# A gate fold in four column groups, with the order of the work computed from new keys

## The chip, the cores and the metric

One core of one Trainium2 chip runs the kernel in one launch. The metric is the device time of that launch in microseconds; less is better. A profile of one execution gives the times of single instructions on the five engines: PE (TensorE; PEld is its weight load), DVE (VectorE), ACT (ScalarE), POOL (GpSimd) and SP (SyncE, which here issues DMAs).

## The reference, cut to what matters

```python
# attention, 2 batches x 8 heads x 768 x 64: a window of 16 around each query and 24 block summaries
x = attention(q, k, v)                                  # 1536 x 512
h = np.maximum(np.maximum(x @ w1, x @ w2), x @ w3)      # 512 -> 768, float64 weights
x2 = h @ w_out                                          # 768 -> 512, float64 weights
# second layer: skip score, 8 experts of 512 -> 1024 -> 512
skip = x2 @ w_skip
e = argmax(x2 @ w_gate); gate = max(softmax(x2 @ w_gate))
out = x2;  out[skip > 0] += gate * (relu(x2 @ m1[e]) @ m2[e])
```

## The kernel before, in words

The tokens are worked in four groups of 384 (u = 0 to 3), each with four pairs of heads (p). For each (u, p) the attention runs scores (sc, `scores`), a reduction on DVE (tt), exponentials on ACT (ex), a reciprocal on DVE (rc), a normalisation on POOL (nm), transposes on PE (tu), a copy (td, on ACT or DVE) and the value product (pv), which ACT and DVE split into a high and a low fp32r part (ph, pl). Each group then has 18 "chains" (c, `chain`, line 413): 12 matmuls each, three products (high by high, high by low, low by high) over four 128-row parts. Their results are combined on ACT and DVE (cd), split on ACT (hh, line 427) and on POOL (hl, line 430), and six f parts of h go into x2 (`x2_mm`, line 440).

The weights of the first layer come as 64-bit floats in 24 pieces (`weight_order`). Each is converted in eight steps: c1 and cq on ACT (lines 385, 381), cb on POOL (line 389), c2, which is two instructions, and c3 on DVE (lines 393, 394, 398), c4, a cast on ACT or POOL (line 402), and c5 on DVE (line 406). Conversion tiles named cx have four slots, and tiles named cr two.

The gate fold. The router needs x2 @ [w_gate, w_skip], ten columns with one of zeros. The kernel puts these columns behind w_out: for each of the six 128-row pieces (3, f) of w_out it computes the 128 x 10 product of that piece with the gate weights, and x2 then has 522 columns. A fold is: `fold_t` (ft), four PE transposes of the piece into PSUM (line 478); `fold_c` (fc), an ACT copy of 128x512 into a cr tile (line 483); `fold_mm` (fm), four matmuls (line 489), each with a transposed 128x128 part as the stationary operand and the ten gate columns (w9) as the moving one, summed in PSUM; `fold_h` (fh, ACT, line 494) and `fold_l` (fl, DVE, line 497), which write the ten columns' high and low parts behind the weights. All six folds must be done before x2 of group 0. The matmul of fm is fp32, and each of the four shows as two instructions in the trace.

The order of the work up to the first expert tile is computed at build time: `arrange` (line 93) walks a list of operations with an engine, a planned duration, predecessors (`after`), buffer slots that an operation takes and gives back (`take`, `uses`), and a key. Whenever an engine is free, the ready operation with the lowest key whose slots are free goes next. The result is the order of each engine's in-order instruction stream; the planned durations and the keys set nothing else. The keys are the table KEYS; one row holds the keys of the folds (f), one those of the 24 conversions (w), one those of the chains (c), one those of the weight loads (l), and so on. The table HOME says which of the movable copies run on which engine: 11 of the 24 c4 casts on POOL, 4 of the 32 td copies on DVE. KIND sorts PE's operations; where two that follow each other are of different kinds, the plan charges PE a small switch.

The PSUM pool psM has three slots, which chains, x2, the transposes and the folds share. The tiles t1 have five slots, and each h tile one. An h tile of group 1 can only be written once x2 of group 0 has read it, so chains of group 1 can run ahead of x2 of group 0 by a few f parts only.

After the planned part (its first expert matmuls are at line 1164) the expert tiles run in an order written out by hand: pairs of tiles (`pair`), single ones (`single`), and a tail tile of 32-token parts (`tail`), whose matmuls (lines 1097 and 1108) have 32 stationary columns and write four column groups of PSUM partitions.

Of the kernel before, what the change touches and what calls it, by code (L numbers as in the profile page):

```python
# [19 lines left out]
P = 128  # L20
# [11 lines left out]
KC1 = DM // P  # L32
FT1 = DF // P
NE, FF = 8, 1024
CAP = 1664
NROW = NE * CAP
NT = B * S // P
SEQ = 24
# [4 lines left out]
MAXT = NT  # L43
ONES, DENSE, OTHER = 32, 64, 128
NRAW = 4
NCON = 293
NG9 = 10
XW = DM + NG9
XA = XW // 2 + 1
# [1 line left out]
TICK, COLUMNS = 10.24 / 3, 3500  # L51
RATE = dict(sc=973, pv=1516, fm=200)
PORT = ("rc", "fk", "c2", "c3", "c5", "tri")
KIND = dict(ch=0, cp=0, x2m=0, sc=1, pv=2, tu=3, st=3, ft=3, fm=1, wu=5)
PORTED, SWITCH = 0.5, 0.06

KEYS = dict(
    s=[[92.73, -181.27, -146.9, -16.72], [12.35, 16.72, 8.44, 74.05], [153.96, 186.16, 209.64, 168.62],
       [133.34, 186.33, 278.0, 31.35]],
    t=[[-48.88, -30.72, -72.46, -64.96], [-115.16, -107.84, -74.91, -96.18], [166.13, 294.76, 153.99, 200.69],  # L60
       [231.34, 228.77, 194.22, 148.78]],
    o=[[-192.26, -99.49, -155.84, -140.77], [18.47, 16.47, 41.51, 37.81], [199.26, 186.19, 169.77, 161.26],
       [233.93, 202.13, 203.99, 188.4]],
    v=[[-76.04, -20.69, -43.67, -52.86], [-21.73, 66.33, 25.77, 62.78], [184.33, 170.84, 129.72, 69.28],
       [217.41, 88.27, 101.06, 155.42]],
    d=[[-190.77, -106.26, -79.61, -70.3], [14.18, 17.1, 46.42, 50.54], [166.48, 205.9, 182.89, 208.26],
       [219.14, 230.09, 253.13, 240.15]],
    e=[[-118.48, -161.65, -267.53, -240.31], [-154.8, -98.57, -105.32, -102.62], [120.29, 131.21, 115.09,
       112.64], [172.38, 173.49, 165.52, 214.6]],
    c=[[23.72, 3.57, 54.8, 22.22, 44.87, 43.88, 88.26, 54.59, 86.07, 36.89, 6.99, -26.57, -32.31, 15.28,  # L70
# [5 lines left out]
    x=[-95.61, 258.36, 184.11, 502.78],  # L76
    w=[18.99, -6.3, 51.7, 43.13, 14.1, 99.04, 74.8, 61.7, 81.52, 99.86, 64.82, 35.29, 63.01, 76.52, 58.72,
       87.44, 90.17, 111.95, 78.35, 139.2, 88.06, 51.57, 155.3, 161.2],
    l=[-91.01, -34.87, 30.81, -0.24, -49.37, 13.11, 15.41, -9.33, 19.62, 18.83, 49.47, 74.71, 132.91, 84.56,
       70.49, 102.42, 139.84, 87.62, 100.63, 192.14, 145.35, 197.7, 185.22, 170.88],  # L80
    f=[61.9, 116.3, 154.03, 120.79, 115.82, 130.96],
)
KEYS = {(z,) + ((n, i) if isinstance(x, list) else (n,)): y for z, v in KEYS.items() for n, x in enumerate(v)
        for i, y in enumerate(x if isinstance(x, list) else [x])}
HOME = {
# [3 lines left out]
}  # L89
HOME = {(n, i): e for (n, e), v in HOME.items() for i in v}  # L90

# [103 lines left out]
def build(tc, a, out):  # L195
    nc = tc.nc
    ctx = ExitStack()
    cp = ctx.enter_context(tc.tile_pool(name="const", bufs=1))
# [22 lines left out]
    KS, VS, XH, XL, WH, WL, HH, HL, LG, X2, ST = ({} for _ in range(11))  # L221
# [264 lines left out]
    def fold_mm(f):  # L486
        pg = psM.tile([P, 512], F32, name="pm")
        for c in range(KC1):
            nc.tensor.matmul(pg[:, :NG9], ST["ft", f][:, c * P:(c + 1) * P], w9[:, c, :], start=(c == 0),  # L489
                             stop=(c == KC1 - 1))  # L490
        ST["fg", f] = pg

    def fold_h(f):
        nc.scalar.copy(WH[3, f][:, DM:], ST["fg", f][:, :NG9])
# [2 lines left out]
        nc.vector.tensor_tensor(WL[3, f][:, DM:], ST["fg", f][:, :NG9], WH[3, f][:, DM:].bitcast(F32), ALU.subtract)  # L497

    con = cp.tile([P, NCON], F32, name="con")
    parts = np.split(np.arange(NCON), np.cumsum([KC1 * NG9, NE, NE, NE, NE * NE, SEQ, NT, 1]))  # L500
    w9, iom, iocap, ione, trie, seqc, tok, quart, tri32 = (con[:, z[0]:z[-1] + 1] for z in parts)
    w9 = w9.rearrange("p (c e) -> p c e", e=NG9)
    trie = trie[:1].rearrange("p (a b) -> p a b", b=NE)
    seqc = seqc[:1]
    tri = cp.tile([P, P], BF16, name="tri")
# [351 lines left out]
    def op(name, eng, dur, key, fn, *args, after=(), take=(), uses=(), lag=0.0):  # L857
        key = (key.name, key.more) if isinstance(key, at) else (None, key)
        busy = eng == "Pool" and lag == 0 and dur > 0 and name[0] != "rs"
        OPS.append(dict(name=name, eng=eng, dur=dur, key=key, fn=fn, args=args, after=after, take=take, uses=uses,  # L860
                        lag=lag, busy=busy))
# [55 lines left out]
    for i in range(20):  # L917
        n = 6 if i == 0 else 3
        op(("wu", i), "PE", 0.216 * n, 1.0 * i, warm_up, n, after=[("wu", i - 1)] if i else [],
           take=[("pm", ("wu", i))] + ([("t1", ("wt",))] if i == 0 else []),  # L920
           uses=[("wu", i)] + ([("wt",)] if i == 19 else []))
    for p in range(NPR):
        att(0, p)
    for n, (j, f) in enumerate(ws):
        t, w = at("w", n), (j, f)
# [8 lines left out]
    for f in range(FT1):  # L934
        t, w = at("f", f), (3, f)
        op(("ft", f), "PE", 0.6, t, fold_t, f, after=[("c3",) + w], take=[("pm", ("ft", f))], uses=[("cx",) + w])
        op(("fc", f), "ACT", 0.48, t + 0.1, fold_c, f, after=[("ft", f)], take=[("cr", ("fc", f))], uses=[("ft", f)])
        op(("fm", f), "PE", 0.9, t + 0.2, fold_mm, f, after=[("fc", f), ("consts",)], take=[("pm", ("fm", f))], uses=[("fc", f)])
        op(("fh", f), "ACT", 0.07, t + 0.3, fold_h, f, after=[("fm", f), ("c4",) + w])
        op(("fl", f), "DVE", 0.1, t + 0.4, fold_l, f, after=[("fh", f), ("c5",) + w], uses=[("fm", f)])  # L940
    for u in range(NG):
        if u + 1 < NG:
# [3 lines left out]
        for k in range(3 * FT1):  # L946
            f, j = divmod(k, 3)
            t, c = at("c", u, k), (u, f, j)
# [4 lines left out]
            for z in range(KC1 - 1 if sp else 0):  # L953
                op(("cp", z) + c, "PE", 0.55, t, chain, u, f, j, [z], after=[("pl", 0, z), ("c5", j, f)] + ([("cp", z - 1) + c] if z else []),
                   take=[] if z else [("pm", ("ch",) + c)])
            if sp:
                dep += [("cp", KC1 - 2) + c]
            op(("ch",) + c, "PE", 0.55 if sp else 2.1, t + 0.01, chain, u, f, j, [KC1 - 1] if sp else range(KC1), after=dep,
               take=[] if sp else [("pm", ("ch",) + c)],
               uses=[("xh", u), ("xl", u)] if k == 3 * FT1 - 1 else [])  # L960
            if j == 0:
                op(("cd",) + c, "ACT", 0.43, t + 0.1, chained, u, f, j, after=[("ch",) + c], take=[("t1", ("t1", u, f))],
                   uses=[("ch",) + c])
            else:
# [15 lines left out]
        if not g3:  # L980
            for t in range(TPG):
                x = x0 + 2 * t
# [5 lines left out]
                else:  # L988
# [3 lines left out]
                   uses=[("x2p", u, t, 0)])  # L992
                op(("xo", u, t, 1), "ACT", 0.28, x + 1.1, x2_out, u, t, 1, after=[d1, ("xo", u, t, 0)])
                op(("lg", u, t), "DVE", 0.1, x + 1.2, x2_lg, u, t, after=[("xo", u, t, 1)] + ([("lg", u, t - 1)] if t else []),
                   uses=[("x2p", u, t, 1)])
                op(("xd", u, t, 0), "DMA", 0.75, x + 1.3, x2_put, u, t, out, after=[("xo", u, t, 1)])
                op(("xd", u, t, 1), "DMA", 0.75, x + 1.4, x2_put, u, t, x2d, after=[("xd", u, t, 0)], uses=[("X2", u, t)])
        else:
            x = x0
            mm(0, 1, 0, x)  # L1000
            d = [mm(0, 1, 1, x + 0.2), mm(1, 1, 2, x + 1), mm(2, 1, 2, x + 2)]
# [421 lines left out]
def host_inputs(inputs):  # L1423
    q, k, v = inputs["q"], inputs["k"], inputs["v"]
    r = {}
# [28 lines left out]
    r["m1"], r["m2"] = inputs["moe2_w1"], inputs["moe2_w2"]  # L1454
    w9 = np.concatenate([inputs["moe2_w_gate"], inputs["moe2_w_skip"][:, None], np.zeros((DM, 1), np.float32)], axis=1)
    w9 = w9.reshape(KC1, P, NG9).transpose(1, 0, 2).reshape(P, KC1 * NG9)
    e = np.arange(NE, dtype=np.float32)
    trie = (e[None, :] < e[:, None]).astype(np.float32)
    same = np.concatenate([e - NE, e * CAP, e, trie.ravel(), np.arange(SEQ, dtype=np.float32)])
    tok = np.arange(B * S, dtype=np.float32).reshape(NT, P).T  # L1460
    quart = (np.arange(P) // TAIL).astype(np.float32)[:, None]
    r["con"] = np.concatenate([w9, np.tile(same, (P, 1)), tok, quart, np.triu(np.ones((P, P), np.float32), 1)], axis=1)
    assert r["con"].shape == (P, NCON)
    return r

# [15 lines left out]
```

## Time and profile before

| what | value |
|---|---|
| median of 3 runs | 456.3 us (454.33 to 458.5) |
| profiled execution, time | 457.91 us |
| its span, first to last instruction | 456.1 us |
| mean granted TensorE clock | 0.984 |
| PE busy | 438.1 us (96%) |
| DVE, ACT, POOL busy | 239.6, 187.1, 141.6 us |

The profiled execution takes 1.8 us more than its span, and 1.6 us more than the median of the runs. A granted clock of 1.00 is 2.4 GHz, 0.50 is 1.2 GHz. Ends of matmuls in the trace are modelled; so the distance between two starts says more about PE than the durations do.

### The profile page before, as it was taken

The numbers are of one execution on the slowest core, as the hardware profiler recorded it, in microseconds if no ns is written. First come the engines' busy times: TensorE is split into PE (matmuls) and PEld (weight loads), VectorE is DVE, ScalarE is ACT, GpSimd is POOL, SyncE is SP. The second block draws the span as 40 slices with busy tenths as digits, with TensorE's granted clock in tenths as the row PEclk, the third lists the DMA queues.
The fourth block names the chain that finished last, engine by engine and source line by source line (L and its number), as shares of the span: only waits on it lengthen the run. The fifth ranks groups of instructions, "written<-read, shape, count | busy, mean of one in ns | idle before, by whom it ended". The sixth has DMA issues, their size and how long they took to land.

```text
span 456.1 us, 9606 instructions
## 1 busy us (share of the span) xinstructions
PE 438.1 (96%) x3546; PEld 396.2 (87%) x3546; DVE 239.6 (53%) x735; ACT 187.1 (41%) x504; POOL 141.6 (31%) x191
## 2 busy tenths in 40 slices
PE   5999899999999998999999999999999999999995
PEld 2767789999999888999999998998999889799875
DVE  3689899999730743315312338658316752221321
ACT  2788887455461575724121126312123521211210
POOL 2464456325211541203320235041326134130400
PEclk9799999999979999999999999999999999999999
DMA  8964735678112346331003038122762184110101
GB/s 246 299 227 130 245 105 177 217 243 282 49 39 92 133 114 151 102 119 47 2 1 139 0 107 311 47 94 47 239 224 93 29 291 148 26 39 13 46 31 49
DMA packets 27585, 56.91 MB, mean 125 GB/s; under 512 B 6099, under 2 KB 8659, under 8 KB 27528
## 3 DMA queue, kind: packets, MB, share of 16 engines
q1 hardware_dynamic: 24968, 50.24, 34.2%
q0 software_dynamic: 2560, 5.96, 4.1%
q8 instruction: 30, 0.49, 0.5%
q14 instruction: 27, 0.22, 0.2%
HBM read 46.69 MB, written 10.47 MB: 125 GB/s over the span
## 4 chain that ended last, share of the span: by engine, by line
PE 83%; DVE 6%; DMA 3%; issue 2%; POOL 1%; ACT 1%; SPq 1%; POOLq 0%; ACTq 0%; DVEq 0%
PE pm L413 27%; PE ph L1164 13%; PE pm L1176 12%; PE pm L440 11%; DMA qt<-in_qt 3%; PE ph L1257 2%; PE po L354 2%; PE pt L341 2%; PE pm L235 2%; PE sc L302 2%; PE pm L489 1%; PE pm L1229 1%; DVE cx L398 1%; PE ptx L776 1%; PE pm L1299 1%
## 5 line engine op out<-in xcount | busy, mean ns | idle before, releaser
L413 PE MATMUL pm<-xh,wh 128*128 128x384 f32 x288 | 65.2, 346 | 0.7 <-DVE t L422 0.4
L413 PE MATMUL pm<-xl,wh 128*128 128x384 f32 x288 | 62.3, 336 | 0.3 <-DVE xl L365 0.3
L413 PE MATMUL pm<-xh,wl 128*128 128x384 f32 x288 | 62.2, 335 | 0.0
L413 PEld LDWEIGHTS pm<-xh,wh 128*128 128x128 f32 x288 | 49.6, 188 | 2.7 <-DVE t L422 1.2
L413 PEld LDWEIGHTS pm<-xl,wh 128*128 128x128 f32 x288 | 51.2, 188 | 0.7 <-DVE xl L365 0.6
L1167 ACT ACTIVATE hth<-ph 128x256 fp32r<-128x256 f32 x40 | 15.3, 384 | 87.6 <-PE ph L1164 81.8
L413 PEld LDWEIGHTS pm<-xh,wl 128*128 128x128 f32 x288 | 51.1, 188 | 0.0
L1168 DVE SCALAR_TENSOR_TENSOR htl<-ph,hth 128x256 fp32r<-128x256 f32 x40 | 16.9, 423 | 57.3 <-ACT hth L1167 57.3
L440 PE MATMUL pm<-wh,h 128*128 128x262 f32 (+1 forms) x288 | 43.4, 292 | 1.8 <-ACT h L427 0.6
L336 POOL TENSOR_TENSOR pr<-pr,se 128x360 f32<-128x360 f32 x32 | 26.5, 845 | 56.2 <-DVE se L332 45.0
L422 DVE TENSOR_TENSOR t<-pm,t 128x384 f32<-128x384 f32 x48 | 26.4, 552 | 32.2 <-PE pm L413 23.0
L326 ACT ACTIVATE pr<-pr,mx 128x120 f32<-128x120 f32 x96 | 36.6, 384 | 15.3 <-DVE mx L319 15.1
L440 PEld LDWEIGHTS pm<-wh,h 128*128 128x128 f32 x288 | 39.0, 195 | 2.9 <-ACT t L420 0.8
L430 POOL TENSOR_TENSOR h<-t,h 128x384 fp32r<-128x384 f32 x24 | 25.8, 1079 | 35.8 <-ACT h L427 25.7
L1176 PE MATMUL pm<-wh,hth 128*128 128x512 f32 x80 | 31.7, 396 | 0.0
L1176 PE MATMUL pm<-wl,hth 128*128 128x512 f32 x80 | 31.5, 393 | 0.0
L1176 PE MATMUL pm<-wh,htl 128*128 128x512 f32 x80 | 31.5, 393 | 0.0
L789 POOL DMA_INDIRECT xn<-x2d,inx x14 | 15.5, 1109 | 45.7 <-DVE xm L1130 30.8
L607 POOL DMA_INDIRECT table<-rtab,rsi x12 | 12.0, 1001 | 55.6 <-DVE g_m L625 20.7
L1164 PE MATMUL ph<-xth,wh 128*128 128x256 f32 x160 | 26.4, 287 | 0.0
L389 POOL TENSOR_SCALAR cx<-cx 128x512 f32<-128x512 f32 x24 | 19.0, 793 | 22.4 <-ACT cx L385 22.1
L1164 PE MATMUL ph<-xtl,wh 128*128 128x256 f32 x160 | 25.7, 282 | 0.0
(333 smaller groups left out, 856.1 us busy)
## 6 DMA issues: line engine op xcount, KB each, us to landing
raw<-in_m SPq DMA_DIRECT2D x48, 256.0 KB
raw<-in_wx SPq DMA_DIRECT2D x22, 512.0 KB
vx<-in_vx SPq DMA_DIRECT2D x14, 288.0 KB
qt<-in_qt SPq DMA_DIRECT2D x16, 192.0 KB
raw<-in_vt SPq DMA_DIRECT2D x8, 384.0 KB
x2d<-raw SPq DMA_DIRECT2D x12, 256.0 KB
kx<-in_kx SPq DMA_DIRECT2D x8, 360.0 KB
out<-raw SPq DMA_DIRECT2D x9, 256.0 KB
```

Of the source, the lines that this page charges most:

```text
L326: nc.scalar.activation(pr[:, t, :], pr[:, t, :], AF.Exp, bias=mx[:, t:t + 1], scale=-1.0, accum_out=se[:, h, t:t + 1])
L336: nc.gpsimd.tensor_tensor(pr, pr, ST["se", u, p][:, h].unsqueeze(2).broadcast_to([P, TPG, KT]), ALU.mult)
L389: nc.gpsimd.tensor_scalar(x, x, HIGH, LOW, ALU.min, ALU.max)
L413: nc.tensor.matmul(ST["ch", u, f, j], l[j, f][:, c * P:(c + 1) * P], r[u][:, c, :], start=(cs[0] == 0 and n == 0), stop=(cs[-1] == KC1 - 1 ...
L422: nc.vector.tensor_tensor(ST["t1", u, f], ps, ST["t1", u, f], ALU.max)
L430: nc.gpsimd.tensor_tensor(HL[u, f], ST["t1", u, f], HH[u, f].bitcast(F32), ALU.subtract)
L440: nc.tensor.matmul(ps, l[u, f][:, t * P:(t + 1) * P], r[3, f][:, lo:hi], start=(part != 1 and n == 0), stop=(part != 0 and n == len(ops) - 1))
L789: nc.gpsimd.indirect_dma_start(out=xn[t], out_offset=None, in_=x2d, in_offset=bass.IndirectOffsetOnAxis(ap=inx[:, t, 0:1], axis=0), bounds ...
L1164: nc.tensor.matmul(ps, w[:, o:o + P], r[:, d, :], start=(n == 0), stop=(n == 3 * KC1 - 1))
L1167: nc.scalar.activation(hh, ps, AF.Relu)
L1168: nc.vector.scalar_tensor_tensor(hl, ps, 0.0, hh.bitcast(F32), ALU.max, ALU.subtract)
L1176: nc.tensor.matmul(py[i], l[:, o:o + P], r, start=(f == 0 and n == 0), stop=(f == 7 and n == 2))
```

## The change

fold_mm swaps the operands: 32 columns of the constants (the ten gate columns of a 128-row part, and 22 columns that follow) are the stationary operand and the transposed piece is the moving one, 128 columns wide. The four parts go to four groups of 32 PSUM partitions, each with a product of its own. A new ACT copy (fs) brings the 128x128 result to the first quarter of the same cr tile, and a new matmul (fq) with a constant 0/1 matrix (pick9, ten more columns of the constants) adds the four parts and turns them to 128 x 10, in another stretch of the same PSUM slot. The cr tile is given back after fq. fh waits for fq in place of fm. The planned durations of the fold change with it, all keys are new, three of the 11 POOL casts go to ACT on balance (five of POOL's move to ACT, two of ACT's to POOL), and td has five copies on DVE in place of four, two of them the same.

```diff
-NCON = 293
+NCON = 303
-KIND = dict(ch=0, cp=0, x2m=0, sc=1, pv=2, tu=3, st=3, ft=3, fm=1, wu=5)
+KIND = dict(ch=0, cp=0, x2m=0, sc=1, pv=2, tu=3, st=3, ft=3, fm=1, fq=1, wu=5)
...
-    w=[18.99, -6.3, 51.7, 43.13, 14.1, 99.04, 74.8, 61.7, 81.52, 99.86, 64.82, 35.29, 63.01, 76.52, 58.72,
-       87.44, 90.17, 111.95, 78.35, 139.2, 88.06, 51.57, 155.3, 161.2],
+    w=[29.12, -32.19, 57.18, 48.36, -2.78, 108.08, 79.78, 61.39, 111.49, 132.7, 74.37, 38.77, 66.75, 74.46,
+       56.98, 94.39, 121.93, 130.7, 84.22, 176.38, 71.77, 45.85, 164.69, 225.48],
...
-    f=[61.9, 116.3, 154.03, 120.79, 115.82, 130.96],
+    f=[60.9, 119.7, 155.29, 122.03, 119.18, 158.31],
...
-    ("c4", "Pool"): [0, 1, 3, 6, 8, 9, 14, 17, 21, 22, 23],
+    ("c4", "Pool"): [0, 1, 3, 6, 8, 16, 19, 22],
     ("fv", "Pool"): [(0, 1), (0, 2), (0, 3)],
-    ("td", "DVE"): [(0, 0, 1), (1, 0, 0), (1, 1, 0), (1, 3, 1)],
+    ("td", "DVE"): [(0, 0, 0), (1, 0, 0), (1, 1, 1), (1, 2, 1), (1, 3, 1)],
...
     def fold_mm(f):
         pg = psM.tile([P, 512], F32, name="pm")
         for c in range(KC1):
-            nc.tensor.matmul(pg[:, :NG9], ST["ft", f][:, c * P:(c + 1) * P], w9[:, c, :], start=(c == 0),
-                             stop=(c == KC1 - 1))
+            nc.tensor.matmul(pg[32 * c:32 * c + 32, :P], con[:, c * NG9:c * NG9 + 32], ST["ft", f][:, c * P:(c + 1) * P], start=True, stop=True)
         ST["fg", f] = pg
+
+    def fold_s(f):
+        nc.scalar.copy(ST["ft", f][:, :P], ST["fg", f][:, :P])
+
+    def fold_q(f):
+        ST["fg", f] = ST["fg", f][:, 2 * P:]
+        nc.tensor.matmul(ST["fg", f][:, :NG9], ST["ft", f][:, :P], pick9, start=True, stop=True)
...
-        op(("fm", f), "PE", 0.9, t + 0.2, fold_mm, f, after=[("fc", f), ("consts",)], take=[("pm", ("fm", f))], uses=[("fc", f)])
-        op(("fh", f), "ACT", 0.07, t + 0.3, fold_h, f, after=[("fm", f), ("c4",) + w])
+        op(("fm", f), "PE", 0.3, t + 0.2, fold_mm, f, after=[("fc", f), ("consts",)], take=[("pm", ("fm", f))])
+        op(("fs", f), "ACT", 0.1, t + 0.22, fold_s, f, after=[("fm", f)])
+        op(("fq", f), "PE", 0.1, t + 0.25, fold_q, f, after=[("fs", f)], uses=[("fc", f)])
+        op(("fh", f), "ACT", 0.07, t + 0.3, fold_h, f, after=[("fq", f), ("c4",) + w])
...
+    pick9 = np.tile(np.eye(32, NG9, dtype=np.float32), (KC1, 1))
```

## Rows read from the trace of the kernel before

**Rows 1.** The page: busy time of each engine, and the granted clock in 40 slices.
```profile
PE 438.1 (96%) x3546; PEld 396.2 (87%) x3546; DVE 239.6 (53%) x735; ACT 187.1 (41%) x504; POOL 141.6 (31%) x191
...
PEclk9799999999979999999999999999999999999999
```

**Rows 2.** Stretches: length, busy time (instructions) by engine, granted clock, DMA share, GB/s.
```profile
40.00:95.00 55.00, 52.89 (x460) 48.55 (x460) 51.57 (x129) 38.87 (x104) 26.67 (x31) 1.00 0.54 181
...
121.00:134.30 13.30, 12.80 (x125) 11.85 (x125) 6.83 (x28) 9.07 (x29) 2.93 (x5) 0.87 0.22 74
...
150.00:217.00 67.00, 64.34 (x682) 60.23 (x682) 31.46 (x147) 37.33 (x122) 19.68 (x25) 1.00 0.38 113
...
sum 258.00, PE 251.23 PEld 240.51 DVE 149.29 ACT 125.68 POOL 81.44; mean PE 41.87 PEld 40.08 DVE 24.88 ACT 20.95 POOL 13.57
...
298.00:456.10 158.10, 151.79 (x1102) 133.56 (x1100) 63.63 (x183) 35.23 (x80) 42.06 (x64) 1.00 0.29 95
```

**Rows 3.** Shorter stretches, the same columns, around the end of the folds.
```profile
130.70:131.00 0.30, 0.30 (x4) 0.21 (x3) 0.00 (x0) 0.30 (x2) 0.00 (x0) 0.53 0.00 0
131.00:136.00 5.00, 5.00 (x42) 4.67 (x41) 1.48 (x13) 2.48 (x11) 0.00 (x0) 0.50 0.01 3
...
137.50:138.00 0.50, 0.50 (x6) 0.50 (x6) 0.00 (x0) 0.00 (x0) 0.38 (x1) 0.95 0.00 0
```

**Rows 4.** The chain of waits in order of time: start, length, what.
```profile
95.35 25.12 PE pm L413 x144
...
128.15 1.69 PE pm L489 x16
...
131.32 1.57 PE pm L489 x8
```

**Rows 5.** Timeline of PE around one fold: start, length, instructions.
```profile
93.70 0.86 PE L413 MATMUL pm<-xh,wl 128*128 128x384 f32 x4
94.40 0.95 PE L489 MATMUL pm<-con,cr 128*128 128x10 f32 x8
95.20 0.95 PE L413 MATMUL pm<-xh,wh 128*128 128x384 f32 x4
```

**Rows 6.** Timeline of PE around a tail product in four column groups (line 1108).
```profile
370.18 0.40 PE L1176 MATMUL pm<-wl,hth 128*128 128x512 f32 x1
370.42 0.40 PE L1176 MATMUL pm<-wh,htl 128*128 128x512 f32 x1
370.78 1.95 PE L1108 MATMUL pm<-raw,hqt 128*32 128x128 f32 x64
372.67 0.74 PE L1164 MATMUL ph<-xth,wh 128*128 128x256 f32 x4
```

**Rows 7.** Lines 1108, 494 and 346: duration in ns (min/median/max); mean for 346.
```profile
L1108 PE MATMUL pm<-raw,hqt x128: 272/273/298, 370.8 to 401.0; 128*32 128x128 f32 x128
...
L494 ACT CAST wh<-pm x6: 164/168/173, 97.0 to 132.9; 128x10 fp32r<-128x10 f32 x6
...
L346 ACT COPY ps<-pt 120x384 f32<-120x384 f32 x28 | 12.6, 478 | 5.2 <-PE pt L341 4.9
```

**Rows 8.** DVE and POOL groups between 40 and 95 us: busy us, mean ns.
```profile
L406 DVE TENSOR_TENSOR wl<-cx,wh 128x512 fp32r<-128x512 f32 x14 | 10.9, 798 | 0.5 <-POOL wh L402 0.5
L394 DVE SCALAR_TENSOR_TENSOR cx<-raw,cx 128x512 int32<-128x512 int32 x13 | 10.6, 813 | 0.4
L393 DVE TENSOR_SCALAR cx<-cx 128x512 int32<-128x512 int32 x14 | 8.0, 573 | 1.1 <-POOL cx L389 1.1
...
L402 POOL CAST wh<-cx 128x512 fp32r<-128x512 f32 x6 | 5.0, 841 | 9.6 <-DVE cx L398 9.6
```

**Rows 9.** The same DVE lines over the whole span: ns min/median/max.
```profile
L406 DVE TENSOR_TENSOR wl<-cx,wh x24: 677/686/1165, 27.5 to 125.4; 128x512 fp32r<-128x512 f32 x24
...
L394 DVE SCALAR_TENSOR_TENSOR cx<-raw,cx x22: 691/694/1195, 22.4 to 122.8; 128x512 int32<-128x512 int32 x22
...
L393 DVE TENSOR_SCALAR cx<-cx x24: 410/420/1235, 22.0 to 122.4; 128x512 int32<-128x512 int32 x24
```

**Rows 10.** Waits of PE: us in total, times, longest.
```profile
PE sc L302 <- DMA qt<-in_qt: 3.2, 4, 1.2
```

More of the change, by code (lines that the diff above doesn't have):

```diff
@@ L53 @@
 PORT = ("rc", "fk", "c2", "c3", "c5", "tri")
-KIND = dict(ch=0, cp=0, x2m=0, sc=1, pv=2, tu=3, st=3, ft=3, fm=1, wu=5)
+KIND = dict(ch=0, cp=0, x2m=0, sc=1, pv=2, tu=3, st=3, ft=3, fm=1, fq=1, wu=5)
 PORTED, SWITCH = 0.5, 0.06
 KEYS = dict(
[L58 to L70, printed above, removed]
[5 rows of a table removed]
-    x=[-95.61, 258.36, 184.11, 502.78],
-    w=[18.99, -6.3, 51.7, 43.13, 14.1, 99.04, 74.8, 61.7, 81.52, 99.86, 64.82, 35.29, 63.01, 76.52, 58.72,
-       87.44, 90.17, 111.95, 78.35, 139.2, 88.06, 51.57, 155.3, 161.2],
-    l=[-91.01, -34.87, 30.81, -0.24, -49.37, 13.11, 15.41, -9.33, 19.62, 18.83, 49.47, 74.71, 132.91, 84.56,
-       70.49, 102.42, 139.84, 87.62, 100.63, 192.14, 145.35, 197.7, 185.22, 170.88],
-    f=[61.9, 116.3, 154.03, 120.79, 115.82, 130.96],
@@ new lines @@
+    s=[[24.03, -85.5, -100.39, -45.22], [13.75, 15.67, -16.33, 40.76], [159.86, 180.48, 245.04, 164.83],
+       [64.44, 269.71, 534.01, -308.07]],
+    t=[[2.77, -10.6, -121.47, -57.55], [-99.04, -88.17, -46.55, -103.34], [186.05, 256.43, 177.98, 197.08],
+       [260.33, 251.89, 264.07, 220.4]],
+    o=[[-170.73, -148.11, -145.47, -165.54], [-34.32, -18.72, -15.45, 22.95], [201.15, 192.21, 127.62, 150.3],
+       [210.15, 135.81, 226.41, 128.81]],
+    v=[[-61.49, 11.46, -21.71, -63.73], [10.04, 80.23, 23.42, 79.38], [177.85, 158.14, 149.56, 32.47],
+       [224.76, 71.15, 50.7, 103.27]],
@@ new lines @@
+    d=[[-227.04, -97.82, -73.51, -69.69], [15.68, 27.29, 34.03, 48.59], [160.72, 218.64, 176.33, 222.71],
+       [246.56, 252.86, 255.07, 257.68]],
+    e=[[-52.47, -139.55, -333.46, -317.98], [-131.33, -94.28, -103.06, -110.59], [117.55, 131.06, 123.86,
+       104.64], [202.12, 153.93, 179.58, 168.86]],
+    c=[[28.76, 7.82, 71.53, 28.8, 53.88, 58.33, 107.65, 72.57, 96.52, 35.49, 18.78, -11.07, -39.83, 14.95,
[5 rows of a table added]
+    x=[-92.05, 267.21, 116.23, 576.71],
+    w=[29.12, -32.19, 57.18, 48.36, -2.78, 108.08, 79.78, 61.39, 111.49, 132.7, 74.37, 38.77, 66.75, 74.46,
+       56.98, 94.39, 121.93, 130.7, 84.22, 176.38, 71.77, 45.85, 164.69, 225.48],
@@ L82 @@
+    l=[-85.03, -43.37, 32.56, 1.33, -47.33, 9.39, 16.12, -11.18, 32.63, 30.52, 69.15, 75.71, 142.35, 80.32,
+       70.11, 104.65, 176.02, 90.34, 99.59, 210.3, 148.8, 205.87, 203.71, 199.22],
+    f=[60.9, 119.7, 155.29, 122.03, 119.18, 158.31],
 )
@@ L499, in build @@
     con = cp.tile([P, NCON], F32, name="con")
-    parts = np.split(np.arange(NCON), np.cumsum([KC1 * NG9, NE, NE, NE, NE * NE, SEQ, NT, 1]))
-    w9, iom, iocap, ione, trie, seqc, tok, quart, tri32 = (con[:, z[0]:z[-1] + 1] for z in parts)
-    w9 = w9.rearrange("p (c e) -> p c e", e=NG9)
+    parts = np.split(np.arange(NCON), np.cumsum([KC1 * NG9, NG9, NE, NE, NE, NE * NE, SEQ, NT, 1]))
+    w9, pick9, iom, iocap, ione, trie, seqc, tok, quart, tri32 = (con[:, z[0]:z[-1] + 1] for z in parts)
     trie = trie[:1].rearrange("p (a b) -> p a b", b=NE)
@@ L1461, in host_inputs @@
     quart = (np.arange(P) // TAIL).astype(np.float32)[:, None]
-    r["con"] = np.concatenate([w9, np.tile(same, (P, 1)), tok, quart, np.triu(np.ones((P, P), np.float32), 1)], axis=1)
+    r["con"] = np.concatenate([w9, pick9, np.tile(same, (P, 1)), tok, quart, np.triu(np.ones((P, P), np.float32), 1)], axis=1)
     assert r["con"].shape == (P, NCON)
```

10 rows, old and new, of the table c are left out of this document.

## The prediction, made before the changed kernel ran

> **What bounds the kernel now.** The page comes first: PE is busy for 438.1 us of a span of 456.1, every other engine for about half of it or less, and the granted clock is full but for two of the 40 slices that show a 7 and a few nines [rows 1]. So what counts is PE time, PE idle time, and time at the lower clock. Then the stretches. From 298 us on, 158.1 us, the order is written by hand and the change leaves it alone; I carry that part over unchanged [rows 2]. The planned part from 40 to 298 us has 258.00 - 251.23 = 6.8 us of idle PE: 2.1 between 40 and 95, 0.5 between 121 and 134.3, 2.7 between 150 and 217, and the rest spread [rows 2]. A new order can win back at most about that much, plus what the clock costs and what modelled ends of matmuls hide.
>
> Three places in it matter. Between 40 and 95 us DVE is busy 51.57 of 55 us, more closely packed than in any later stage: the weight conversion sets the pace, PE is fed as pieces come [rows 2]. Between 121 and 134.3 us five of the six folds run; the chain of waits passes through line 489 twice there, for 1.69 and 1.57 us [rows 4]. And the clock is at its lower level from about 130.7 to 137.5 us, 6.8 us at half speed, right behind that crowd of folds: it falls while PE is busy without a pause, but with instructions that stream ten columns each, and it rises again when x2 has run for three microseconds [rows 3]. At half speed 6.8 us do the work of 3.4, so 3.4 us are lost there. Last, scores waited for their query tile four times, 3.2 us in all [rows 10].
>
> **The fold on PE.** Six folds, one after another. Old price: the eight instructions of a fold start at 94.40 and the next chain at 95.20, so 0.80 us, or 0.10 per instruction, with chains of the same array shape on both sides [rows 5]. Six make 4.8 us.
>
> New price. The trace of before has the same shape of product (128 rows, 32 stationary columns, 128 moving ones, four column groups): the tail's line 1108. 64 such instructions and what follows them take 372.67 - 370.78 = 1.89 us [rows 6]. That is 0.03 us an instruction, far below their single duration of 0.27 [rows 7], so four groups do run beside each other. But the change of shape is not free. Into it: line 1176 starts every 0.23 to 0.24 us, so the next start was due at about 370.65 and came at 370.78, 0.13 late [rows 6]. Out of it: the last of the 64 ends at 372.73 by the trace (start and length of the group) and the next product starts at 372.67 [rows 6], so the next shape starts only when the last 0.27 us product is nearly over: about 0.2 us more than the 0.03 of the pitch. With pitch (1.89 - 0.21) / 63 = 0.027, fm costs 0.13 + 7 x 0.027 + 0.21 = 0.53 us. fq is one product of the old kind, two instructions at 0.10, so 0.20 [rows 5]. New fold: 0.73 against 0.80, and six save 0.4 us. The good end leaves the shape change out, because an fm may stand beside another fm or products that change shape anyway: 8 x 0.03 + 0.20 = 0.44, six save 2.2 us. The bad end has a change of shape around fq as well and nothing shared: 0.73 + 0.33 = 1.06, six cost 1.6 us more. I take 0.4 saved, since chains and transposes with full 128 columns are what stands around most folds.
>
> A rule of the Trainium skill speaks against the change here: TensorEngine Tiling (Array Packing), section Key Properties, says that a change of tiling mode, not merely of tile, drains TensorE. The trace agrees, with 0.13 us in and about 0.2 out [rows 6]. The same page, section When to Use Tiling, advises just this swap of operands with fourfold column tiling where the moving side has 32 columns or fewer; taken alone, its factor of four would make fm 0.80 / 4 = 0.20, and six folds would save 2.4 us with fq (an estimate from that page and rows 5).
>
> **The fold beside PE.** ACT gets six more copies, 128x128 out of PSUM. No such copy is in the trace; 10 columns take 0.168 us and 384 take 0.478 [rows 7], and those are the bounds; by the line through them 128 columns take 0.27, six 1.6 us. ACT is busy 9.07 of 13.3 us in the stretch of the folds [rows 2], so mostly this lies beside other work. What can be on the path is latency: fq waits for fs, fh for fq, so each fold's way to x2 is longer by 0.27 for fs, some 0.3 for fq and two hand-overs, about 0.8 us. Within the crowd other folds cover it; behind the last fold nothing does but scores and transposes. I charge 0.3 us. If the cover is gone it is 0.8 once, and for all five in turn 4 us (a rival). Behind a waiting fq in PE's in-order stream stand other folds, scores, and then x2 of group 0, for which everything waits. The wider constants are ten columns in 303: nothing.
>
> **The clock.** The new folds stream 128 columns where the old streamed ten, and the crowd is shorter. What is left of it has the same transposes and scores, and a PE that waits for fs looks idle. Bounds: the fall goes (-3.4 us), or it comes back and lasts a further 3.4 us at half speed (+1.7). I take half of the gain, -1.7, because what came before the fall is worked on from both sides.
>
> **The order.** The keys of the folds stay nearly as they were (60.9, 119.7, ... where 61.9, 116.3, ... stood), so the crowd of five stays behind the chains of group 1; the last conversions get later keys (161.2 to 225.48). Net three c4 casts leave POOL for ACT. POOL and DVE hinder each other here: between 40 and 95 us three DVE lines average 798, 813 and 573 ns [rows 8] where their shortest take 677, 691 and 410 [rows 9]. That is 14 x 0.121 + 13 x 0.122 + 14 x 0.163 = 5.6 us of DVE lost beside 26.67 us of POOL work [rows 2], 0.21 us for each us of POOL. Three casts of 0.84 us [rows 8] free 0.5 us of DVE; ACT, at 38.87 of 55 us, has room. For a plan made with such overlaps in mind I take another 1.0 us. Together -1.5, about a quarter of the 6.8 us of idle PE. Bounds: -4, if 40 to 95 us loses nearly all its idle time and the waits for query tiles go too; +3, if the new order only moves the waits elsewhere, as it can, since the keys are for a plan and not for a trace.
>
> **Sum.** -0.4 (folds on PE) + 0.3 (latency) - 1.7 (clock) - 1.5 (order) = -3.3 us. The profiled execution of 457.91 us would become 454.6. It lies 1.6 us above the median, so the median of 456.3 becomes **453.0**.
>
> **The rivals.**
> *Faster than that.* Folds stand together or beside other changes of shape (-2.2), the low clock goes altogether (-3.4), and the order wins 2 us with latency covered: -7.6, so 448.7. For it: all three terms are in the rows, and PE in the stretch of the folds was bound by its own work. Against it: the price of changing shape [rows 6].
> *The swap as the page's factor of four.* Only the fold gains, with no drain, -2.4, and order and clock give nothing: 453.9. The drain in rows 6 speaks against it; its time cannot be told from the forecast's, so its chance is inside "same".
> *Nothing.* The folds save 0.4, the clock falls as before, and the order is as good as the old one: 456.
> *Slower: the folds wait in a ring.* The cr tile is now held through fs and fq. Two cr slots serve five folds. While x2 of group 0 has not run, h tiles are not free and chains of group 1 can't fill PE. If PE's stream has fq close behind its fs, PE stands still for fs plus two hand-overs, some 0.8 us, five times, 4.0 us; idle PE then keeps the clock low for another 6.8 us or so at half speed in part (+1.7), and the order gives nothing: +5.7 - 0.4, so 461.6. It decides if PE's idle time between fm and fq exceeds about 0.3 us on average. Against it: 13.3 us for five folds is 2.7 us each, and the order may put other folds between.
>
> **How the numbers follow.** Forecast 45%, faster rival 27%, nothing (with the page's factor) 16%, slower 12%. A measurement of this kernel tells about 1% from no change, 4.6 us, here 451.7 and 460.9. Faster by over 1%: most of the faster rival (0.24) and a fifth of the forecast's chance (0.09), 0.33. Slower by over 1%: the slower rival, 0.12. The rest, 0.55. The forecast's own range is 450 to 456. The full range runs from 447 (-2.2 - 3.4 - 4 and some latency) to 459.5 (+1.6 on folds and +1.6 net from order and clock), with the far half of the slower rival left out.
>
> **What would show it.** In the changed profile: fm's eight instructions some 0.03 us apart with a start-to-start time of about 0.5 us to the next chain; two instructions of fq in about 0.2; an fs of 0.27. The stretch from the first of the crowded folds to x2 of group 0 should go from 13.3 to about 11 us; a low clock of less than 6.8 us behind it; DVE lines 406, 394 and 393 shorter on average than in rows 8; idle PE from 40 to 298 us near 5 us. I am wrong if the part before the first expert tile (298 us) shortens by less than 1 us or more than 6, if PE idles before fq, or if the part behind it changes by more than 1 us.

## The result and the profile after

The changed kernel takes 450.81 us (median of 18 runs, 449.15 to 454.85) where the kernel before measured beside it took 455.95: a ratio of 0.9902, interval 0.9874 to 0.9931. Two later measurements gave 0.9926 (0.9889 to 0.9962) and 0.9917 (0.9884 to 0.9949), so it is about 4 us faster. The forecast was 3.3 us less, a median of 453.0. Medians are those of all runs, while a ratio leaves out runs over 1.5% above the fastest of their kernel and is not the quotient of the two medians. The profiled execution takes 451.38 us, its span is 449.6.

The page of the changed kernel: busy time, and the granted clock in 40 slices. The low slice behind the folds [rows 1] is gone in this execution; the one near the start is still there.

```profile
PE 432.4 (96%) x3558; PEld 389.2 (87%) x3558; DVE 236.7 (53%) x736; ACT 189.5 (42%) x512; POOL 136.9 (30%) x188
...
PEclk9799999999999999999999999999999999999999
```

Stretches of the changed kernel, cut at the same points of the work as far as the new order has them (columns as in rows 2):

```profile
40.00:91.50 51.50, 51.31 (x464) 47.77 (x463) 50.45 (x130) 41.20 (x108) 22.51 (x27) 1.00 0.62 207
...
117.00:132.00 15.00, 13.74 (x174) 11.20 (x174) 9.74 (x54) 13.86 (x51) 4.41 (x7) 1.00 0.20 66
...
145.50:208.20 62.70, 59.02 (x635) 54.28 (x634) 28.38 (x133) 34.41 (x110) 18.03 (x22) 1.00 0.39 121
...
293.10:449.60 156.50, 150.48 (x1101) 132.59 (x1099) 63.74 (x183) 35.26 (x80) 41.97 (x64) 0.99 0.30 96
```

Four things answer to [rows 2]. In the conversion stage PE idles 0.2 us, not 2.1. In the stretch of the folds it idles 1.3, not 0.5, with twelve more chain products and a set of 24 score products more in the stretch. Between 145 and 208 us it idles 3.7 us; from 150 to 217 it was 2.7. And the expert part, which the change does not touch, takes 156.5 us in place of 158.1.

The chain of waits shows the first and the last of these. The long run of 144 chain products begins at 91.52 us, 3.8 us earlier than in [rows 4], with the same products of PE ahead of it in both kernels (229 chain products, 192 value products and one fold from the start of the span); 36 expert products take 4.24 us:

```profile
91.52 25.15 PE pm L413 x144
...
316.36 4.24 PE ph L1171 x36
```

The folds on PE (timeline: start, length, instructions; line 489 is fm, 497 is fq):

```profile
118.67 0.64 PE L489 MATMUL pm<-cr,con 128*32 128x128 f32 x16
119.53 0.39 PE L497 MATMUL pm<-con,cr 128*128 128x10 f32 x2 [0.22 <-ACT cr L493]
119.78 0.63 PE L478 MATMUL pm<-ident,cx 128*128 128x128 f32 x4
...
121.88 0.86 PE L413 MATMUL pm<-xh,wl 128*128 128x384 f32 x4
122.67 0.43 PE L489 MATMUL pm<-cr,con 128*32 128x128 f32 x8
123.02 0.32 PE L260 MATMUL pm<-ident,vs 128*120 128x128 f32 x1
...
129.14 0.61 PE L497 MATMUL pm<-con,cr 128*128 128x10 f32 x4 [0.65 <-ACT cr L493]
```

A single fm was due at 121.88 + 4 x 0.174 = 122.58, began at 122.67, and the next product began at 123.02: 0.44 us with both changes of shape, where the forecast had 0.53. Two fms side by side take 0.64, only 0.21 more than one, so they share those changes. An fq takes 0.25 (119.53 to 119.78). Twice PE waits for fs on ACT, 0.22 and 0.65 us; an fs itself takes 0.27 us, as forecast. Around the single fm 0.09 us are lost on the way in, and from the last start of its products (122.67 + 0.43 - 0.27 = 122.83) it is 0.19 us to the next start. TensorEngine Tiling (Array Packing) of the Trainium skill, section Key Properties, has TensorE drained at a change of tiling mode; the trace agrees, with time lost on both sides of fm.

The lines of rows 8 in the changed kernel, from 40 to 91.5 us:

```profile
L406 DVE TENSOR_TENSOR wl<-cx,wh 128x512 fp32r<-128x512 f32 x14 | 11.0, 794 | 0.0
...
L394 DVE SCALAR_TENSOR_TENSOR cx<-raw,cx 128x512 int32<-128x512 int32 x12 | 9.6, 799 | 0.4
L393 DVE TENSOR_SCALAR cx<-cx 128x512 int32<-128x512 int32 x14 | 7.7, 548 | 0.0
```

They are hardly shorter than before (794 for 798, 799 for 813, 548 for 573 ns). What went are the gaps between them: DVE waited 1.1 us at line 393 for POOL's line 389 [rows 8], and now waits for nothing there.

Last, what the new order lost. The timeline of POOL between 160 and 171 us:

```profile
160.31 0.98 POOL L612 DMA_INDIRECT table<-rtab,rsi  x1 [4.60 <-DMA table<-rtab,rsi]
161.31 1.01 POOL L430 TENSOR_TENSOR h<-t,h 128x384 fp32r<-128x384 f32 x1
166.74 0.99 POOL L612 DMA_INDIRECT table<-rtab,rsi  x1 [4.41 <-DMA table<-rtab,rsi]
167.75 3.02 POOL L336 TENSOR_TENSOR pr<-pr,se 128x360 f32<-128x360 f32 x4
```

and the longest of PE's waits from 146 to 210 us (sum, count, longest, in us):

```profile
PE pt L341 <- POOL pr L336: 2.6, 2, 2.4
```

The third scatter of group 0 (line 612) stands at the head of POOL's in-order stream and waits for the landing of the second one; four normalisations stand behind it, and PE stands still for 2.4 us for the first of them. Not every execution shows this: in the third profile of the changed kernel the longest such wait is 2.1 us, in the second one 0.5, with 1.8 us of waiting for a query tile instead.

### The profile page after: what moved, and what is told of

The parts are those of the page before. It is cut to its first block, busy times and chain, and to the rows that moved or that the text cites. A ratio compares the mean times of both kernels' runs of the same rounds, so it can differ in the third digit from the quotient of the medians.

```text
span 449.6 us, 9647 instructions
## 1 busy us (share of the span) xinstructions
PE 432.4 (96%) x3558; PEld 389.2 (87%) x3558; DVE 236.7 (53%) x736; ACT 189.5 (42%) x512; POOL 136.9 (30%) x188
## 4 chain that ended last, share of the span: by engine, by line
PE 82%; DVE 6%; ACT 5%; issue 2%; DMA 2%; POOL 1%; SPq 1%; POOLq 0%; DVEq 0%; ACTq 0%
PE pm L413 31%; PE ph L1171 13%; PE pm L1183 12%; PE pm L440 9%; PE ph L1264 2%; PE pt L341 2%; PE po L354 2%; ACT pr L326 2%; PE sc L302 2%; DMA qt<-in_qt 2%; PE pm L235 1%; PE pm L1236 1%; DVE wl L814 1%; PE pm L1306 1%; PE ptx L781 1%
## 5 line engine op out<-in xcount | busy, mean ns | idle before, releaser
L440 PEld LDWEIGHTS pm<-wh,h 128*128 128x128 f32 x288 | 38.0, 189 | 2.6 <-ACT x L462 1.0
L389 POOL TENSOR_SCALAR cx<-cx 128x512 f32<-128x512 f32 x24 | 17.5, 733 | 30.4 <-ACT cx L385 26.8
```

Source lines behind the costliest of these rows:

```text
L389: nc.gpsimd.tensor_scalar(x, x, HIGH, LOW, ALU.min, ALU.max)
L440: nc.tensor.matmul(ps, l[u, f][:, t * P:(t + 1) * P], r[3, f][:, lo:hi], start=(part != 1 and n == 0), stop=(part != 0 and n == len(ops) - 1))
```

## The experiments

Parts of the change alone, a control of addresses, further profiles of both kernels, and two moves that repair what the order lost. Each ratio is to the kernel before, measured beside that kernel on the same chip.

**Order alone.** The changed order with the old fold in it.

```diff
-            nc.tensor.matmul(pg[32 * c:32 * c + 32, :P], con[:, c * NG9:c * NG9 + 32], ST["ft", f][:, c * P:(c + 1) * P], start=True, stop=True)
+            nc.tensor.matmul(pg[:, :NG9], ST["ft", f][:, c * P:(c + 1) * P], con[:, c * NG9:(c + 1) * NG9], start=(c == 0),
+                             stop=(c == KC1 - 1))
...
     def fold_s(f):
-        nc.scalar.copy(ST["ft", f][:, :P], ST["fg", f][:, :P])
+        pass
...
     def fold_q(f):
-        ST["fg", f] = ST["fg", f][:, 2 * P:]
-        nc.tensor.matmul(ST["fg", f][:, :NG9], ST["ft", f][:, :P], pick9, start=True, stop=True)
+        pass
```

> The changed kernel's order, keys and engines, with the old fold in it: four products of ten moving columns where fm stands, nothing where fs and fq stand. Theory A (order and fold give about half each): the stage up to the 219th chain product keeps its 3.6 us, but the crowd of folds is PE-bound again, 5 x 0.3 = 1.5 us longer, and the low clock comes back behind it for 6.8 us (3.4 us lost). The first expert product comes at about 293.1 + 1.8 + 3.4 = 298 us, the ratio to the kernel before is about 0.997 with the tail's gain. Theory B (the clock is kept by the order, not by the fold): no low clock behind the folds; 293.1 + 1.8 = 295 us, ratio about 0.993. Theory C (the fold gives nothing): 293 us, ratio 0.990.

Measured: 453.01 us, ratio 0.9975 (0.994 to 1.001). The chain of waits has

```profile
86.59 29.29 PE pm L413 x168
```

that is, the long run begins two chains (24 products, 4.2 us) earlier, the equivalent of 90.8 us for the last 144 of it: the gain of the conversion stage is the order's. No low clock stands behind the folds, although all six are the old ones; a low stretch of 3.4 us stands at about 170 us instead, where PE waited for POOL. So in this execution theory B's mechanism held for the clock, while theory A's time came out (0.997): the order lost most of what it won in the conversion stage again, in the stretch of the folds and behind 146 us.

The same order with the old and the new fold also prices the fold. From the first transposes of the crowd to the first product of x2, with the same 24 chain products and 72 score products and a full clock, first order alone, then the changed kernel (columns as in rows 2):

```profile
115.70:132.03 16.33, 15.66 (x167) 13.84 (x166) 10.11 (x54) 12.71 (x44) 4.42 (x7) 1.00 0.18 60
```

```profile
116.49:131.79 15.30, 14.04 (x176) 11.35 (x175) 10.05 (x54) 13.65 (x49) 4.41 (x7) 1.00 0.20 64
```

Five new folds save 1.0 us there, their waits for fs included.

**Fold alone.** The changed fold with the old keys and engines. The order is computed from these keys for the new list of operations, so it is not the old order: 24 chain products stand among its folds where the old order has 12.

```diff
 KEYS = dict(
...
-    f=[60.9, 119.7, 155.29, 122.03, 119.18, 158.31],
+    f=[61.9, 116.3, 154.03, 120.79, 115.82, 130.96],
...
-    ("c4", "Pool"): [0, 1, 3, 6, 8, 16, 19, 22],
+    ("c4", "Pool"): [0, 1, 3, 6, 8, 9, 14, 17, 21, 22, 23],
...
-    ("td", "DVE"): [(0, 0, 0), (1, 0, 0), (1, 1, 1), (1, 2, 1), (1, 3, 1)],
+    ("td", "DVE"): [(0, 0, 1), (1, 0, 0), (1, 1, 0), (1, 3, 1)],
```

> The changed fold with the old keys and the old engines of the casts; the order is computed from the old keys with the new operations. Theory A: the fold brings 1.8 us on PE and keeps the clock (3.4 us), the conversion stage stays as slow as before; with the tail's 1.5 us the ratio is about 0.987 to 0.990. Theory B: keys that were found for another list of operations lose what the fold gains; the ratio is 0.995 or above, and the loss sits in stages with no fold in them. Theory C: the low clock stays, since the crowd of folds is as poor in columns as before; ratio about 0.993.

Measured: 453.1 us, ratio 0.9946 (0.9916 to 0.9977). Between theories A and B: faster than before, but not by what was forecast for it. The conversion stage is as slow as before: in this kernel's stretches PE idles 2.0 us there, and the clock was low for part of it, 0.97 on average.

```profile
40.00:94.20 54.20, 52.22 (x449) 48.35 (x448) 51.48 (x125) 38.67 (x103) 25.97 (x30) 0.97 0.55 176
```

No low clock stands behind its folds, so theory C fell in this execution. One of its fms stands between scores and a chain:

```profile
122.48 0.43 PE L489 MATMUL pm<-cr,con 128*32 128x128 f32 x8
122.84 0.97 PE L413 MATMUL pm<-xh,wh 128*128 128x384 f32 x4
```

0.36 us: seven steps of the forecast's 0.027 and the 0.19 of the way out make 0.38, so nothing is left for a way in. The scores ahead of it have another shape than a chain has; that this is the reason is likely, but not shown.

**The casts' engines.** The changed order, with the c4 casts where they were before.

```diff
-        COPY[HOME.get(("c4", ws.index((j, f))), "ACT")](WH[j, f][:, :512], ST["cx", j, f])
+        COPY["Pool" if ws.index((j, f)) in (0, 1, 3, 6, 8, 9, 14, 17, 21, 22, 23) else "ACT"](WH[j, f][:, :512], ST["cx", j, f])
```

> The changed kernel with its order, but the c4 casts on the engines of the kernel before: five go from ACT back to POOL and two from POOL to ACT. Theory A: the 3.6 us won between 40 and 95 us come from the order of the conversions, and the casts' engines matter little: the 219th chain product ends within 1 us of the changed kernel's, and the ratio stays at 0.989 to 0.993. Theory B: they come from fewer POOL casts beside DVE: DVE lines 406, 394 and 398 get longer, the stage loses 2 us or more, ratio 0.995 or above.

Measured: 451.23 us, ratio 0.9916 (0.9881 to 0.9952). The long run of chain products begins at 91.33 us, within 0.2 of the changed kernel:

```profile
91.33 25.15 PE pm L413 x144
```

Line 394 does get longer (847 ns for 799), but the stage hardly does: beside order alone with its 90.8, which like this profile has a full clock in the first 40 us, it is 0.5 us later. Theory A: the order of the conversions brought the gain, and the casts' engines some 0.5 us of it at most.

**The expert part and the addresses.** Unused columns in the constants of the kernel before, ten and then two.

```diff
-NCON = 293
+NCON = 303
...
-    parts = np.split(np.arange(NCON), np.cumsum([KC1 * NG9, NE, NE, NE, NE * NE, SEQ, NT, 1]))
+    parts = np.split(np.arange(NCON), np.cumsum([KC1 * NG9, NE, NE, NE, NE * NE, SEQ, NT, 1, P]))
...
```

The second run has 295 columns in place of 303.

> The kernel before with ten unused columns added to the constants, nothing else. The part after the first expert product is 1.5 us shorter in the changed kernel (157.9 to 156.5 us), and line 1164 (1171 there) starts every 0.118 us instead of 0.120. Theory A: the wider constants move every tile allocated after them, and the expert weights are then read faster as stationary operands. Then this kernel shows a pitch of 0.118 for line 1164, an expert part of 156.5 us and a time 1.5 us below the kernel before (ratio 0.997). Theory B: the expert part differs from one execution or chip to the next, or follows from what the planned part left behind. Then the pitch stays 0.120 and the ratio is 1.000.

> The kernel before with two unused columns in the constants, which move no other tile: the first weight tile stays at byte 20608 of its partition, where ten columns moved it to 20640 and left the moving operand xth at 208864. If the shorter expert part is a matter of these addresses, this kernel has the old pitch of 0.120 us at line 1164 and an expert part of 157.9 us or a little more; if any edit of the constants does it, 0.118 and 156.5.

Ten columns: 455.09 us, ratio 0.9971 (0.993 to 1.0013), its span 452.2. Two columns, profiled once: a span of 450.3. The chains of waits, first with ten, then with two:

```profile
319.00 4.24 PE ph L1164 x36
```

```profile
339.13 4.32 PE ph L1164 x36
```

With ten columns the pitch of line 1164 is 0.118 us, with two it is 0.120 as in the kernel before. From the first expert product to the end it is 452.2 - 295.6 = 156.6 us with ten and 450.3 - 292.1 = 158.2 with two. That is 1.6 us, but not all of it is the pitch: 480 products with 0.002 us less are some 0.9 us. The rest is one wait in the tail, where PE's transposes of hq wait for ACT. It stands in the kernel before and in the copy with two columns, not with ten columns and not in the first profile of the changed kernel, but in its second and third profiles again. The changed kernel, first and second profile:

```profile
391.28 0.38 PE L1109 MATMUL pm<-ident,hq 128*128 128x128 f32 x2
```

```profile
392.73 0.44 PE L1109 MATMUL pm<-ident,hq 128*128 128x128 f32 x2 [0.47 <-ACT hq L1106]
```

In these two later profiles the pitch is 0.118 and the expert part takes 157.4 and 157.3 us. So 0.9 us of the result go with ten columns: they move the expert weights by 32 bytes (20608 to 20640 for the first) against xth, which stays at 208864, and two columns move neither. The other 0.6 us come and go at the same addresses. The time alone, at 0.3% with an interval of 0.4%, would not have shown it.

**Second profiles of both kernels, and the clock.** No edit.

> The kernel before, unaltered, for a second profile. If the low clock behind the folds is a matter of the moment, this profile may have it elsewhere or not at all, and its length at the start may differ; if the order fixes it, it lies from about 130.7 to 137.5 us again. The conversion stage (40 us to the 219th chain product) loses 4.5 us of PE time under both.

> The changed kernel once more, with nothing altered, beside the experiments of this call and for a second profile. Theory A (the low clock behind the folds is a matter of the moment at which the execution starts, as the padded kernel's full clock there suggests): the low stretches in this profile need not lie where they lay in the first one; the conversion stage again loses about 1 us and the stage from 146 to 210 us about 7 us of PE time. Theory B (the clock follows the order alone): the same stretches at the same places. Ratio 0.990 under both.

> The changed kernel, unaltered, as the neighbour of the run before: ratio 0.990 to 0.993 to the kernel before; its third profile shows a conversion stage that loses 1 to 1.7 us and a stage from 146 to 210 us that loses about 7.

The kernel before showed its low clock behind the folds again (130 to 140 us, mean 0.74):

```profile
130.00:140.00 10.00, 10.00 (x81) 9.66 (x82) 2.01 (x16) 3.60 (x17) 1.54 (x2) 0.74 0.04 13
```

With two unused columns the same instructions in the same order had none:

```profile
130.00:140.00 10.00, 10.00 (x100) 9.84 (x98) 2.01 (x16) 3.88 (x17) 1.53 (x2) 1.00 0.15 54
```

and with ten columns none either. In the old order, then, it falls there in two profiles of four, both of them without added columns. The changed kernel has none behind the folds in three, but its third profile has one between 160 and 180 us, behind its wait for POOL:

```profile
160.00:180.00 20.00, 17.68 (x193) 15.78 (x189) 6.53 (x44) 13.88 (x50) 7.56 (x9) 0.83 0.28 79
```

A mean of 0.83 over 20 us is a loss of 3.4 us, as much as behind the old folds. First expert products came at 298.0 and 296.0 us in the kernel before, 295.6 and 292.1 in its padded copies, and 293.0, 293.6 and 295.6 in the changed kernel. A single pair of profiles therefore says little about differences under 5 us of this kernel. The start of the long run is steadier: 95.35, 93.47, 95.25 and 93.25 in the old order, 91.52, 92.12 and 91.64 in the new one, 2.6 us between the means. The clock of the first 40 us moves it too, but among profiles with the same mean clock there the new order is always earlier: 95.35 and 91.52 us at 0.91, 95.25 and 92.12 at 0.87, 93.47 or 93.25 and 91.64 at 0.96.

Profiles are few, but every run has its span and its mean granted clock on record, and span x (1 - clock) estimates what it lost against a full clock: for the profile of rows 1 it is 456.1 x 0.016 = 7.3 us, 3.4 of them behind the folds. Of 75 runs of the kernel before, 13 lost less than 3.4 us in all. So the low clock behind the folds is not in every execution of the unaltered kernel either. The means over the runs that the ratios use:

| kernel | runs | lost to the clock, us | the kernel before beside it, us |
|---|---|---|---|
| changed, second and third measurement | 12, 12 | 4.7, 4.1 | 5.7, 5.2 |
| changed, the casts' engines of before | 10 | 2.8 | 5.8 |
| fold alone | 10 | 3.2 | 5.8 |
| order alone | 10 | 5.0 | 5.8 |
| new steps without their cover (next) | 10 | 6.6 | 5.7 |

With standard errors of 0.3 to 0.6 us on each mean, the kernels with the new fold and its cover lose 1.0 to 2.9 us less; the 2.6 and 2.9 are clear of the noise, the 1.0 and 1.1 of the changed kernel itself only just when taken together, and the 0.8 of the order alone is not. Where in the span the clock was regained the means do not say, since the low stretch near the start differs as well.

**New steps without their cover.** fs and fq straight behind fm.

```diff
         ST["fg", f] = pg
+        nc.scalar.copy(ST["ft", f][:, :P], ST["fg", f][:, :P])
+        ST["fg", f] = ST["fg", f][:, 2 * P:]
+        nc.tensor.matmul(ST["fg", f][:, :NG9], ST["ft", f][:, :P], pick9, start=True, stop=True)
...
     def fold_s(f):
...
+        pass
```

> The changed kernel with fs and fq straight behind fm, in place of where the plan put them: the cover that other work gives between fm and fq is taken away. Theory A (latency of the new steps is hidden by the order): PE idles some 0.6 us before each fq, 3 to 4 us over six folds, most of it in the crowd before x2 of group 0; ratio 0.997 or above. Theory B (other work of that stage is late by as much anyway, such as the last conversions or scores): under 1 us is lost; ratio 0.990 to 0.992.

Measured: 458.63 us, ratio 1.0066 (1.0034 to 1.0097): slower than the kernel before. The first of PE's waits for a fold (columns as above):

```profile
PE pm L493 <- ACT cr L491: 3.1, 6, 0.8
```

and two of the second products in PE's timeline:

```profile
118.85 0.39 PE L493 MATMUL pm<-con,cr 128*128 128x10 f32 x2 [0.44 <-ACT cr L491]
...
124.12 0.39 PE L493 MATMUL pm<-con,cr 128*128 128x10 f32 x2 [0.77 <-ACT cr L491]
```

Theory A. PE stands still before every fq, 0.5 us on average, 3.1 in all. Beside the changed kernel measured with it (453.22) the median is 5.4 us higher. This profile is of the quickest of the ten runs (454.87); in it the stretch from the first transposes of the crowd to x2, with the work of the two stretches under "Order alone", takes 4.4 us longer than the changed kernel's 15.30:

```profile
115.80:135.46 19.66, 16.22 (x176) 12.93 (x175) 10.20 (x54) 15.14 (x57) 4.41 (x7) 0.91 0.16 50
```

Of that 2.2 us are more idle time of PE (3.4 for 1.3) and 1.7 are the clock (19.66 x 0.09); the last half microsecond was not traced.

**Repairing the order.** The third scatter of group 0 moved behind the four normalisations, and then the logit copies of group 3 between the last expert splits as well.

```diff
-        for o in arrange(OPS, room, KEYS):
+        order = list(arrange(OPS, room, KEYS))
+
+        def later(name, past):
+            names = [o["name"] for o in order]
+            o = order.pop(names.index(name))
+            order.insert([o["name"] for o in order].index(past) + 1, o)
+        later(("rs", 0, 2), ("nm", 3, 0, 1))
+        later(("lg", 3, 0), ("s1", 8))
+        later(("lg", 3, 1), ("s1", 10))
+        later(("lg", 3, 2), ("s1", 13))
+        for o in order:
```

The first run has the first of the four moves alone.

> The changed kernel with one instruction moved: the third scatter of group 0 (line 612) stands behind the normalisations of u = 2, p = 3 and u = 3, p = 0 in POOL's stream, where it stood before them. In the changed kernel it waits 4.4 us for the scatter before it and PE waits 2.4 us for the normalisations behind. Theory A (this in-order wait is what the new order lost between 146 and 210 us): PE's wait on POOL at line 341 goes, the stage loses some 5 us as in the kernel before and not 7, and the ratio is about 0.985. Theory B (something else comes last there, query tiles or exponentials on ACT): the wait moves to another releaser and the ratio stays at 0.990.

> As the run with the scatter moved, and the three logit copies of group 3 (line 453) stand between the last expert splits on DVE, where they stood behind all of them. In the changed kernel PE idles 0.8 us before x2's second half, because a PSUM slot waits for those copies. Theory A: this wait goes and the first expert product comes 0.5 to 0.8 us earlier than with the scatter alone; ratio about 0.983. Theory B: the splits that come later hold up the first expert products instead; ratio as with the scatter alone.

> The changed kernel with the scatter and the three logit copies moved, a second time, beside the changed kernel itself in the same call. If the two moves are worth what the profiles showed (1 us between 146 and 210, 0.3 at the hand-over), it is 1 to 2.5 us faster than the changed kernel; if the earlier difference was the spread of the runs, the two are within 0.5 us.

Measured: scatter alone 450.89 us, 0.9889 (0.9842 to 0.9936); both 450.77, 0.9892 (0.9846 to 0.9938), beside the changed kernel's 453.22; both again 449.89, 0.9889 (0.984 to 0.9937), beside 451.75. PE's waits from 146 to 210 us with the scatter moved:

```profile
PE po L354 <- issue: 1.2, 1, 1.2
PE pm L585 <- DVE t L422: 1.0, 1, 1.0
PE sc L302 <- DVE xl L365: 0.6, 1, 0.6
PE sc L302 <- DMA qt<-in_qt: 0.4, 1, 0.4
```

The wait for POOL is gone from the list, and others of 1.2 and 0.6 us stand there in its place: theory A for the mechanism, theory B for part of the sum. The two moves together are 2.4 and 1.9 us below the changed kernel in two measurements, though the intervals of the ratios overlap. No version here has a lower ratio. Moving the logit copies adds nothing that the times show, as theory B of that run has it.

## Why the prediction was right, step by step

**The total** was -3.3 us and came out at -3.4 to -4.5. Part of that is luck: terms that were off in both directions cancelled.

**The fold on PE** was sized at -0.4. With fm at 0.36 to 0.44, less where two share the changes of shape, and fq at 0.25 or below, a fold costs some 0.55 and not 0.73 us; six save about 1.5 of 4.8. The mechanism (a change of shape that costs more than the products) was right; the step that failed in size was "chains and transposes with full 128 columns are what stands around most folds": the plan put fms side by side and next to scores. One reading was short as well: among the five crowded folds the chain of waits of the kernel before passes line 489 four times and not twice, for 5.0 us, with these two pieces beside those of rows 4:

```profile
122.54 0.99 PE pm L489 x8
...
125.75 0.79 PE pm L489 x8
```

**Latency** was +0.3; PE waits 0.9 us for fs in the changed kernel. The slower rival's place and mechanism are shown by the tight version; its condition (fq close behind fs) was not met because the order has other work between.

**The clock** was taken at half of 3.4 us. Over the whole span the runs with the new fold and its cover lost 1.0 to 2.9 us less to it, with the forecast's 1.7 in the middle. The reason given, folds that stream more columns, is not shown: old folds had a full clock behind them in two of four profiles of the old order and in the one of the new order, and the changed kernel has a low stretch elsewhere in one profile of three. Nor did the clock of [rows 3] fall during folds: at 130.7 us PE had been in transposes for 1 us.

```profile
127.98 1.85 PE L489 MATMUL pm<-con,cr 128*128 128x10 f32 x16
129.69 0.64 PE L478 MATMUL pm<-ident,cx 128*128 128x128 f32 x4
130.16 0.94 PE L341 MATMUL pt<-ident,pr 128*120 128x128 f32 x6
```

**The order** was -1.5, from 0.5 for casts and 1.0 for the plan, in the conversion stage. The stage gained 2.6 us, nearly all of it by order and some 0.5 at most by the casts' engines. DVE's lines there were to become shorter and hardly did; the gaps between them went. The stretch from the first crowded fold to x2 was to go from 13.3 to about 11 us, and it did not. Without its 12 more chain products (2.1 us) and 24 more score products (0.8) the changed kernel's 15.30 us are 12.4, as long as the old order takes at a full clock, here with two unused columns:

```profile
118.20:130.64 12.44, 11.84 (x130) 10.74 (x128) 7.32 (x28) 9.12 (x29) 2.94 (x5) 1.00 0.24 78
```

So the new order lost there the 1.0 us that the new fold won. Between 145 and 210 us about 1 us of PE idle time came back, more where the clock fell behind the wait. The upper bound of the order ("only moves the waits elsewhere") is thus partly true. That idle PE from 40 us to the first expert tile would go from 6.8 to near 5 us was wrong: it stays at about 6.8.

**The expert part** was carried over unchanged, and this is the step that failed outright: ten columns of constants, costed at nothing, took 0.9 us out of it by addresses. The prediction named a change of over 1 us there as a sign of being wrong. The first pair of profiles shows 1.5, of which 0.6 is the wait in the tail; the later profiles of the changed kernel (157.4, 157.3) lie 0.7 to 1.0 below the two of the kernel before (158.1, 158.3).

By these sizes the sum is -2.6 (conversion stage) + 0 (stretch of the folds, with fold, fs and order) + 1 (behind 145 us) - 0.9 (addresses) = -2.5 us without the clock, and -3.5 with the 1.0 of the second measurement, against a measured -3.4 to -4.5. How the time divides between fold and order is not resolved by the times themselves: each alone, addresses included, gave 0.9946 and 0.9975 with intervals of 0.3% on either side, from medians of 453.10 and 453.01 us, and the ten unused columns alone gave 0.9971.

## What to carry to other kernels

Swapping operands so that a product streams 128 columns in four column groups paid here only with other work beside the extra steps: in the same new order the time was 0.7 to 1% below the old kernel's with the copy and the second product spread among other work, and 0.7% above it with them straight behind. An in-order queue must not hold an instruction that waits for a transfer ahead of work that another engine needs. And when an edit adds even a few columns to an early buffer, compare the parts that it doesn't touch, in more than one profile: here a shift of addresses was 0.9 of some 4 us, and a wait of 0.6 us that came and went looked like part of it.

## What was not expected of the hardware

Products of 128 rows and 256 columns went from a pitch of 0.120 to 0.118 us, 0.9 us over the expert part, in every profile with ten more columns of constants, where the weights lie at 20640 and not at 20608 and the moving operand stays at 208864; two columns that move nothing left the pitch at 0.120. Why 32 bytes do this, no run shows. And the granted clock fell to 1.2 GHz at a given place in some executions of a kernel and not in others, for 6.8 us behind the old folds and for 3.4 us near 170 us in the run of the order alone. By their clocks, runs of the kernel before lost between 0.5 and 11.9 us to it, which is much of their spread from 450.8 to 460.7 us.
